# Two heads' rows in one transfer, and both pairs of batches through the first three layers before the last two

## The chip, the cores and the metric

The program runs on one core of one Trainium2 chip. The metric is the device time of one execution in microseconds. The kernel before has a median of 1160.0 us over three runs (1157.83 to 1166.39). The execution that was profiled took 1158.56 us, and its trace spans 1156.8 us of that. The mean clock granted to TensorE over the span was 0.984 of full speed.

## The reference

Inputs are float32, and the product accuracy asked for is close to float32's. Four batches of 448 tokens, 12 heads of 64:

```
scores = q @ k.T / sqrt(64) - log(448);  x = sigmoid(scores) @ v     # per batch and head
x  = x / sqrt(mean(x*x) + 1e-6) * rms_g                              # [1792, 768]
x  = (silu(x @ w_gate) * (x @ w_val)) @ w_out                        # 768 -> 1536 -> 768
h  = x @ w_in;   out = (h - tanh(h)) @ w_out2                        # 768 -> 2048 -> 768
```

The weights arrive as 64-bit words, which the kernel itself turns into float32 on the chip.

## The kernel before, in words

**Numbers in two parts.** A float32 operand is split into a high part (the value rounded to the matmul format fp32r) and a low part (value minus high part). A product of two operands is three matmuls: high by high, high by low, low by high. The splits are a cast (L279, on ScalarE "ACT" or VectorE "DVE") and a subtraction (L418, L459, L530, L670, L708, on DVE or GpSimd "POOL").

**Stages.** Attention comes first, pair of heads by pair of heads (24 pairs). For a pair, `pair_load` issues its DMAs, `pair_prep` splits q and k, `scores` makes the scores (L553), `sigmoid` runs on ACT (L563), `pair_av` multiplies with v (L593, L599). After each batch, `norm` makes the row norms. Then come the five weight matrices, called phases: Ag and Av (gate and value, L794), B (out, L830), C (in of the second block, L794), D (out of the second block, L830). All of this is done for batches 0 and 1, and then once more for batches 2 and 3.

**Jobs.** A and C phases use Strassen's seven products in Winograd's form on 2 by 2 blocks, where the two block columns are the two batches. One job is 63 matmuls. Its left factors are sums of weight blocks, made by `factors` (L413 the sums, L279 and L418 the splits). Its right factors are the sums B11, T1, T2, T3, B21, T4, B22 of pieces of x, made by `right_units` (L675 the sums, L670 the splits) for `i` = 0, 1, 2, each from two pieces m = 2i and 2i+1 of both batches. B and D phases are plain: a block is 6 matmuls, a group is four k by six m, so 24 blocks or 144 matmuls. In each group m goes up, and for each m the four k of the group come one after another. Each A and C job ends in evictions (L765) and the activation (L742, L743 for the gate; L746; L750, L751 for tanh), and then a split (L708) that gives one k for B or D. The evictions of B and D are L721.

**Weights.** `load` fetches 768 KB of raw words (L317). `convert` turns them into float32 by three ACT steps (L333, L338, L342; L336 on DVE instead of L338 in places) and two joins (L345 on DVE or POOL, L347 on DVE). Converted tiles are stored to DRAM for the second pair of batches and fetched from there (`fetch`, L392, L396). Six tiles of A are converted early, beside the attention. All the others of A, B, C and D are converted just ahead of the job that uses them, all within the passes of batches 0 and 1.

**What sets the order.** No engine queue is written by hand. The kernel records units of work in program order with `plan.add`, each with its engines, a guessed duration, what it reads and writes, and `after`, the guessed time from the end of a DMA's issue to its landing. `Plan.issue` then simulates the engines with these guesses. Of the units that could start within 300 ns of the soonest, it takes the one recorded first, and so writes one fixed instruction list per engine. At run time each engine works its list strictly in order and waits where an operand is late. All DMAs are issued by one engine, SyncE ("SP"). Buffers come from pools. The pool `wt` has 8 buffers, shared by raw words (at most 2), converted tiles (`whole` at most 2, `whl` at most 3) and left factors (`op`, at most 6).

**Second pair.** The attention output of batches 2 and 3 is spilled to DRAM (L623) and read back by `reload_x` (L662) during the last D group of batches 0 and 1. Beside that group, `right_a` also applies the norm (L697) and makes the right factors of the next A jobs.

Of the kernel before, what the change touches and what calls it, by code (L numbers as in the profile page):

```python
# [21 lines left out]
P = 128  # L22
# [4 lines left out]
GR = 4  # L27
# [9 lines left out]
N_UNIT, N_MOE, N_WT, N_CV = 81, 44, 8, 5  # L37
# [8 lines left out]
ORDER_1_OUT = [(k, m) for g in range(KF1 // GR) for m in range(KM) for k in range(g * GR, (g + 1) * GR)]  # L46
ORDER_2 = [(k, m) for m in range(KF2) for k in range(KM)]
ORDER_2_OUT = [(k, m) for g in range(KF2 // GR) for m in range(KM) for k in range(g * GR, (g + 1) * GR)]
# [13 lines left out]
class Plan:  # L62
# [7 lines left out]
    def __init__(self, room):  # L70
        self.room, self.work = room, []

    def add(self, engines, run, reads=(), writes=(), stream=None, after=0):

        n = len(self.work)
        self.work.append((engines, run, tuple(reads), tuple(writes), stream, after))
        for s, _ in (*reads, *writes):
            if not s.uses or s.uses[-1] != n:
                s.uses.append(n)

    def issue(self):
# [70 lines left out]
        while len(issued) < n_work:  # L152
# [25 lines left out]
            finish, start, n, e, ns, uses_port = min((c for c in cands if c[1] <= soonest), key=lambda c: c[2])  # L178
# [33 lines left out]
def tile_sigmoid_attention_moe_moe(  # L212
# [31 lines left out]
        "cv": (N_CV, {"cv": 2, "c": 2, "top": 1, "a22": 2}),  # L244
# [47 lines left out]
    for bs in BATCHES:  # L292
        for names, ph, n, order in ((FIRSTS[0], "B", KF1 // GR, ORDER_1_OUT), (FIRSTS[1], "D", KF2 // GR, ORDER_2_OUT)):
# [6 lines left out]
    early = [(ph, p) for ph, bs, p, blocks in jobs if blocks is None][:N_EARLY]  # L300


    turns = []
    for ph, p in early:
        turns += [(ph, 2 * p), (ph, 2 * p + 1)]
    for ph, bs, p, blocks in jobs:
        if bs == BATCHES[0] and (ph, p) not in early:
            turns += [(ph, p)] if blocks else [(ph, 2 * p), (ph, 2 * p + 1)]
# [3 lines left out]
    def load(i, reads=()):  # L312
# [4 lines left out]
        add({"SP": (2200, False)}, lambda e: nc.sync.dma_start(out=r.tile, in_=SRC[ph][at]), reads, [r["l"], r["h"]], after=2000)  # L317

    def convert(ph, at, word, c, x):
# [24 lines left out]
        def join():  # L344
            add({**dve(NW, fast=True), **pool1(NW)}, lambda e: ENG[e].tensor_scalar(  # L345
# [37 lines left out]
    def fetch(i):  # L383
# [4 lines left out]
        if blocks:  # L388
            if bs == BATCHES[0]:
                return  # L390
            d, w = stored.pop((ph, at)), slot("whl", wt_p, [P, 2, NW], F32R, "wt")
            add({"SP": (2200, False)}, lambda e: nc.sync.dma_start(out=w.tile.bitcast(F32), in_=d.tile), [d[x] for x in "hl"], [w["h"], w["l"]], after=2000)  # L392
            whls[i] = w
        elif bs == BATCHES[1] or (ph, at) in early:
# [51 lines left out]
    def whole_tile(i):  # L446

        ph, _, at, _ = jobs[i]
        c = slot("c", cv_p, [P, NW], U32, "cv")
# [481 lines left out]
    for j in range(len(jobs)):  # L931
        fetch(j + BACK)
        ahead = conv(j + AHEAD)
        for n, u in enumerate(job_units(j)):
# [8 lines left out]
            for f in ahead[lo:hi]:  # L943
                f()
# [60 lines left out]
```

## Time and profile before

| | |
|---|---|
| median of 3 runs | 1160.0 us (1157.83 to 1166.39) |
| profiled execution | 1158.56 us, span 1156.8 us |
| TensorE (PE) busy | 1107.9 us, 96% |
| VectorE (DVE) busy | 865.2 us, 75% |
| ScalarE (ACT) busy | 558.2 us, 48% |
| GpSimd (POOL) busy | 321.9 us, 28% |
| DMA | 162.27 MB, mean 140 GB/s |

A busy PE is not a PE at full pace. Matmuls overlap, so the pace is best read from how many stand in a stretch, and lost time from the spots where the next one starts late.

### The profile page before, as it was taken

To read this page: it belongs to the slowest core of one execution; us is meant where nothing else is said; L and a number is where in the kernel's file an instruction comes from. 1 tells how busy PE (TensorE), PEld (TensorE's weight loads), DVE (VectorE), ACT (ScalarE), POOL (GpSimd) and SP (SyncE) were. 2 spreads that over 40 slices of the span, in tenths; PEclk is the share of its full clock that TensorE was granted. 3 is DMA by queue.
4 is the path that set the end of the run, shared out by engine and by line. 5 is a ranking of instruction groups with operands and counts; after the bars stand their busy time and mean duration, and the time that the engine had idled before them with its cause. 6 is when DMAs were issued, how large, how long until landed. Compare 5 with 4: busy or idle time off the path is not lost. (4 is left out here: it accounts for less than half of the span.)

```text
span 1156.8 us, 15127 instructions
## 1 busy us (share of the span) xinstructions
PE 1107.9 (96%) x5574; PEld 943.8 (82%) x5574; DVE 865.2 (75%) x1347; ACT 558.2 (48%) x904; POOL 321.9 (28%) x203
## 2 busy tenths in 40 slices
PE   8798988999999997999999899999999999999998
PEld 4344443989999986899999789999999899999987
DVE  2566883796698899898999899948838899394642
ACT  4678996455476576676575424312303243121110
POOL 0003010253254232334444523322211324051300
PEclk9898999999999999999999899999999999999999
DMA  3777655234257463455556651221313113313203
GB/s 105 228 216 235 195 152 190 91 109 164 82 191 269 141 232 123 138 211 198 207 211 216 241 189 56 83 82 55 110 55 110 55 56 109 104 61 110 109 1 123
DMA packets 55322, 162.27 MB, mean 140 GB/s; under 512 B 13904, under 2 KB 30928, under 8 KB 55248
## 3 DMA queue, kind: packets, MB, share of 16 engines
q1 hardware_dynamic: 55248, 161.30, 41.4%
q8 instruction: 44, 0.72, 0.3%
q14 instruction: 30, 0.25, 0.1%
HBM read 115.27 MB, written 46.01 MB: 139 GB/s over the span
## 5 line engine op out<-in xcount | busy, mean ns | idle before, releaser
L794 PE MATMUL ps<-unit,wt 128*128 128x448 f32 x2160 | 454.9, 368 | 11.2 <-DVE unit L670 7.0
L794 PEld LDWEIGHTS ps<-unit,wt 128*128 128x128 f32 x2160 | 407.8, 189 | 49.6 <-DVE unit L670 7.8
L830 PE MATMUL ps<-unit,wt 128*128 128x448 f32 x2016 | 416.6, 367 | 8.2 <-DVE unit L279 7.3
L830 PEld LDWEIGHTS ps<-unit,wt 128*128 128x128 f32 x2016 | 379.7, 189 | 42.8 <-DVE unit L279 8.4
L765 DVE TENSOR_TENSOR unit<-ps,unit 128x448 f32<-128x448 f32 x240 | 142.6, 618 | 47.5 <-PE ps L794 44.0
L279 ACT COPY unit<-ps 128x448 f32<-128x448 f32 x86 | 45.8, 534 | 162.5 <-PE ps L794 90.0
L279 ACT CAST unit<-unit 128x448 fp32r<-128x448 f32 (+1 forms) x143 | 76.9, 567 | 86.0 <-DVE unit L721 22.0
L721 DVE TENSOR_TENSOR unit<-ps,unit 128x448 f32<-128x448 f32 x120 | 68.9, 616 | 60.9 <-PE ps L830 60.8
L345 POOL TENSOR_SCALAR cv<-cv 128x768 f32<-128x768 f32 x28 | 82.6, 2948 | 89.1 <-ACT cv L342 89.1
L563 ACT ACTIVATE unit<-ps 128x448 f32<-128x448 f32 x192 | 90.2, 543 | 5.4 <-PE ps L553 4.1
L279 ACT CAST wt<-cv 128x768 fp32r<-128x768 f32 x78 | 64.6, 833 | 57.2 <-PE ps L794 20.8
L553 PE MATMUL ps<-unit 64*128 64x448 f32 (+1 forms) x576 | 75.7, 397 | 14.3 <-ACT unit L279 5.0
L553 PEld LDWEIGHTS ps<-unit 64*128 64x128 f32 (+1 forms) x576 | 52.1, 182 | 42.9 <-issue 18.8
L794 PE MATMUL ps<-unit,cv 128*128 128x448 f32 x360 | 79.8, 366 | 0.0
L593 PE MATMUL ps<-unit 128*64 128x448 f32 x288 | 68.2, 607 | 9.3 <-ACT unit L563 9.2
L794 PEld LDWEIGHTS ps<-unit,cv 128*128 128x128 f32 x360 | 67.5, 188 | 5.6
L708 DVE TENSOR_TENSOR unit<-unit 128x448 fp32r<-128x448 f32 x89 | 66.5, 757 | 4.3 <-ACT unit L279 2.3
L418 POOL TENSOR_TENSOR wt<-cv,wt 128x768 fp32r<-128x768 f32 x21 | 41.6, 1980 | 100.2 <-ACT wt L279 56.7
L279 DVE CAST unit<-unit 128x448 fp32r<-128x448 f32 (+1 forms) x102 | 48.2, 473 | 28.2 <-DMA unit<-in_qkt 25.4
L342 ACT ACTIVATE cv<-wt 128x768 f32<-128x768 f32 x68 | 61.5, 906 | 10.5 <-DVE cv L347 3.9
L708 POOL TENSOR_TENSOR unit<-unit 128x448 fp32r<-128x448 f32 x23 | 26.8, 1169 | 138.0 <-DVE unit L279 130.2
L418 DVE TENSOR_TENSOR wt<-cv,wt 128x768 fp32r<-128x768 f32 x59 | 62.1, 1064 | 2.5 <-ACT wt L279 1.5
(71 smaller groups left out, 1020.7 us busy)
## 6 DMA issues: line engine op xcount, KB each, us to landing
wt<-in_w_out SPq DMA_DIRECT2D x28, 768.0 KB, 4.9
wt<-in_w_in SPq DMA_DIRECT2D x16, 768.0 KB, 5.9
wD<-wt SPq DMA_DIRECT2D x16, 768.0 KB, 4.1
wt<-wD SPq DMA_DIRECT2D x16, 768.0 KB, 4.2
wt<-in_w_gate SPq DMA_DIRECT2D x12, 768.0 KB, 5.4
wt<-in_w_val SPq DMA_DIRECT2D x12, 768.0 KB, 5.8
wB<-wt SPq DMA_DIRECT2D x12, 768.0 KB, 4.0
wt<-wB SPq DMA_DIRECT2D x12, 768.0 KB, 4.1
```

What stands on the lines that cost most here:

```text
L279: add(engines, lambda e: (nc.scalar.copy if e == "ACT" else nc.vector.tensor_copy)(to(), of()), reads, writes)
L342: add(act(NW), lambda e: nc.scalar.activation(t.tile, r.tile[:, :, 1].bitcast(F32), AF.Abs, scale=2.0 ** 16), [r["h"]], [t["t"]])
L345: add({**dve(NW, fast=True), **pool1(NW)}, lambda e: ENG[e].tensor_scalar(out=t.tile, in0=t.tile, scalar1=LOW, scalar2=HIGH, op0=ALU.max, ...
L418: add({**dve(n, psum=False), **pool(n)}, lambda e: ENG[e].tensor_sub(lo(), a(), hi().bitcast(F32)), [*ak, kh], [kl])
L553: nc.tensor.matmul(ps[i, c].tile[:n, :S], lhsT=f[w].tile[rows, c * P:c * P + n], rhs=f[q].tile[rows, :], start=(w, q) == ("kh", "qh"), sto ...
L563: add(act(S, psum=True), lambda e: nc.scalar.activation(to.tile[at:at + n, :S], ps.tile[:n, :S], AF.Sigmoid, bias=-math.log(S), scale=1.0 ...
L593: nc.tensor.matmul(ps.tile[i * D:(i + 1) * D, :S], lhsT=v.tile[:, n * D:(n + 1) * D], rhs=a.tile, start=(c == 0), stop=False)
L708: add({**pool(S), **dve(S, psum=False)}, lambda e: ENG[e].tensor_sub(c["l"].tile, t.tile, c["h"].tile.bitcast(F32)), [t["t"], kh], [kl])
L721: add(dve(S), lambda e: nc.vector.tensor_add(a.tile, psv(), a.tile), [ps["t"], a["t"]], [a["t"]])
L765: add(dve(S), lambda e: nc.vector.tensor_add(t.tile, banks[n].tile[:, :S], x.tile), [banks[n]["t"], x["t"]], [t["t"]])
L794: nc.tensor.matmul(ps.tile[:, :S], lhsT=part(a), rhs=x[b].tile, start=n not in ON_TOP and i == 0 and q == 0, stop=i == 2 and q == 2, skip_ ...
L830: nc.tensor.matmul(ps.tile[:, :S], lhsT=wt, rhs=a[p].tile, start=first and i == 0, stop=last and i == 2,)
```

## The change

The same numbers are computed, and the number of matmuls is the same. The parts:

1. **Loads of a pair of heads.** q and k of the two heads lie one after the other in DRAM, and now come as one DMA over 128 partitions instead of two over 64. Only the last 64 columns of k stay two DMAs in batches 0 and 1. v takes one DMA, its end one. A pair has 6 issues in batches 0 and 1 (9 before), 4 in batches 2 and 3 (10 before).
2. **Raw words.** The guess `after` of a raw load goes from 2000 to 3500 ns. The first raw loads no longer wait for the split of a pair.
3. **Order of phases.** Before: A and B, then C and D, for batches 0 and 1, then the same for 2 and 3. Now: A, B (0, 1), A, B (2, 3), C, D (2, 3), C, D (0, 1). The output of B for batches 0 and 1 is spilled and read back.
4. **Conversion of C.** All eight tiles of C are converted and stored beside the second pass of A and B (`later`, `steps`). D is converted in the pass of batches 2 and 3.
5. **Last group of B and D.** For m = 0 to 2 the first two k come for all three m, then the other two; m = 3 to 5 as before (`out_order`).
6. **Right factors after B.** `right_units` is cut in two parts, and for C these units rank 60 places earlier in the planner's choice. The first job of a phase does all products of i = 0 and 1 (save the one on top of another's bank) before any of i = 2.
7. **Silu.** The gate's sigmoid and multiplication become one Silu on ACT. The first limit of a conversion (L345) is on DVE alone. The pool `unit` has 79 buffers (81), `cv` 6 (5), of kind `c` 1 (2).

```
+FIRST = 60
+LEAD = {"A": BATCHES[0], "B": BATCHES[0], "C": BATCHES[1], "D": BATCHES[1]}
+def out_order(n):
+    half = GR // 2
+    order = [(k, m) for g in range(n // GR - 1) for m in range(KM) for k in range(g * GR, (g + 1) * GR)]
+    order += [(k, m) for ks in (range(n - GR, n - half), range(n - half, n)) for m in range(KM // 2) for k in ks]
+    return order + [(k, m) for m in range(KM // 2, KM) for k in range(n - GR, n)]
...
+        self.rank.append(n + self.lag)
-            finish, start, n, e, ns, uses_port = min((c for c in cands if c[1] <= soonest), key=lambda c: c[2])
+            finish, start, n, e, ns, uses_port = min((c for c in cands if c[1] <= soonest), key=lambda c: (self.rank[c[2]], c[2]))
...
-    for bs in BATCHES:
-        for names, ph, n, order in ((FIRSTS[0], "B", KF1 // GR, ORDER_1_OUT), (FIRSTS[1], "D", KF2 // GR, ORDER_2_OUT)):
+    for names, ph, n, order in ((FIRSTS[0], "B", KF1 // GR, ORDER_1_OUT), (FIRSTS[1], "D", KF2 // GR, ORDER_2_OUT)):
+        for bs in (LEAD[ph], *(x for x in BATCHES if x != LEAD[ph])):
...
+    first = [bs == LEAD[ph[0]] for ph, bs, _, _ in jobs]
+    early = FIRSTS[0][:N_EARLY]
+    later = FIRSTS[1]
...
-        add({"SP": (2200, False)}, lambda e: nc.sync.dma_start(out=r.tile, in_=SRC[ph][at]), reads, [r["l"], r["h"]], after=2000)
+        add({"SP": (2200, False)}, lambda e: nc.sync.dma_start(out=r.tile, in_=SRC[ph][at]), reads, [r["l"], r["h"]], after=3500)
...
-            add({**dve(NW, fast=True), **pool1(NW)}, lambda e: ENG[e].tensor_scalar(
+            add(dve(NW, fast=True), lambda e: ENG[e].tensor_scalar(
...
+            apart = w == "k" and hi > 3 * P and b < PAIRED
+            for i in range(2 if apart else 1):
+                rows = slice(i * D, (i + 1) * D) if apart else slice(0, P)
+                of = qk_rows[h * P + D:][rows, at + i * D:at + i * D + hi - lo]
...
+        if part == 0:
+            return [begin] + split("B11", "T1")
+        return [sums] + split("T2", "T3") + [rest] + split("B21", "T4", "B22")
...
-                xg[b, m] = a
-                if b % 2 and m % 2:
-                    for u in right_units("C", (b - 1, b), m // 2, xg):
+                xs[b, m] = xg[b, m] = a
+                if b not in LEAD["C"]:
+                    spill(b, m)
+                elif b % 2:
+                    plan.lag = -FIRST
+                    for u in right_units("C", (b - 1, b), m // 2, xg, m % 2):
                         u()
+                    plan.lag = 0
...
-            add(act(S, psum=psum), lambda e: nc.scalar.activation(sg.tile, of(), AF.Sigmoid), [x["t"]], [sg["t"]])
-            add(two, lambda e: ENG[e].tensor_mul(sg.tile, of(), sg.tile), [x["t"], sg["t"]], [sg["t"]])
+            add(act(S, psum=psum), lambda e: nc.scalar.activation(sg.tile, of(), AF.Silu), [x["t"]], [sg["t"]])
...
-    beside = [(last_c + 1, half_way, right_a(BATCHES[1], True))]
+    steps = [f for ph, p in later for f in both_halves(ph, p)]
+    beside = [(last["A"] + 1, starts["A", BATCHES[1]] - 1, right_all("A", BATCHES[1], True)),
+              (last["C"] + 1, starts["C", BATCHES[0]] - 1, right_all("C", BATCHES[0], True)),
+              (starts["A", BATCHES[1]], starts["C", BATCHES[1]] - 2, steps)]
```

What the planner makes of it is shown at three places. First ACT's list in the attention, from the second pair on. `L563 ACTIVATE` (`L585` in the changed kernel) are sigmoids, `L333` (`L345`) is the first step of a conversion, which needs raw words that have landed. Before:

```order
L279 COPY unit<-ps 128x448
L612 ACTIVATE unit<-unit 128x448
L563 ACTIVATE unit<-ps 128x448 x2
L563 ACTIVATE unit<-ps 64x448 x2
L563 ACTIVATE unit<-ps 128x448 x4
L279 COPY unit<-ps 128x448
L612 ACTIVATE unit<-unit 128x448
L333 ACTIVATE wt<-wt 128x768
```

Now:

```order
L585 ACTIVATE unit<-ps 128x448 x2
L585 ACTIVATE unit<-ps 64x448 x2
L585 ACTIVATE unit<-ps 128x448 x4
L291 COPY unit<-ps 128x448
L632 ACTIVATE unit<-unit 128x448
L585 ACTIVATE unit<-ps 128x448 x2
L585 ACTIVATE unit<-ps 64x448 x2
L585 ACTIVATE unit<-ps 128x448 x4
L345 ACTIVATE wt<-wt 128x768
```

The first conversion step stood behind 20 sigmoids and now stands behind 28, one pair later.

Second, SP's list at the start of the program, the first pair of heads. Before:

```order
L500 DMA unit<-in_qkt 64x128 x2
L500 DMA unit<-in_qkt 64x448 x2
L500 DMA unit<-in_qkt 64x256 x2
L500 DMA unit<-in_qkt 64x64 x2
L511 DMA unit<-in_vp 128x384
L520 DMA ve<-in_vp 64x64 x2
```

Now:

```order
L522 DMA unit<-in_qkt 128x128
L522 DMA unit<-in_qkt 128x448
L522 DMA unit<-in_qkt 128x256
L522 DMA unit<-in_qkt 64x64 x2
L540 DMA unit<-in_vp 128x384
L542 DMA ve<-in_vp 128x128
```

Eleven issues became seven. The first raw load stood behind 32 issues of q and k and now stands behind 21, after the same pair of heads.

Third, DVE's list where the last evictions of B (`L721`, now `L757`) lead to the right factors of C (`L675` and `L670`, now `L698` and `L693`). `L345`, `L347`, `L413` and `L418` are conversion and left factors. Before, for batches 0 and 1:

```order
L721 TENSOR_TENSOR unit<-ps,unit 128x448 x2
L345 TENSOR_SCALAR cv<-cv 128x768
L347 SCALAR_TENSOR_TENSOR wt<-cv,wt 128x768
L413 TENSOR_TENSOR cv<-wt 128x384
L413 TENSOR_TENSOR cv<-cv,wt 128x384
L413 TENSOR_TENSOR cv<-wt 128x384
L413 TENSOR_TENSOR cv<-wt,cv 128x384
L418 TENSOR_TENSOR wt<-wt 128x768
L675 TENSOR_TENSOR unit<-unit 128x448 x3
L670 TENSOR_TENSOR unit<-unit 128x448 x7
```

Now, for batches 2 and 3:

```order
L425 TENSOR_TENSOR cv<-wt,cv 128x384
L693 TENSOR_TENSOR unit<-unit 128x448
L430 TENSOR_TENSOR wt<-wt 128x768
L430 TENSOR_TENSOR wt<-cv,wt 128x2x384
L757 TENSOR_TENSOR unit<-ps,unit 128x448 x2
L698 TENSOR_TENSOR unit<-unit 128x448 x3
L693 TENSOR_TENSOR unit<-unit 128x448 x5
```

Seven DVE steps stood between the last evictions and the sums that C waits for, and now none does.

## Rows read from the trace of the kernel before

**Rows 1.** Stretches from start:end us (attention, first A+B, C+D, second A+B); columns as named

```profile
core 0: us, PE busy (x) PEld busy (x) DVE busy (x) ACT busy (x) POOL busy (x), PEclk, DMA share, GB/s
0.00:203.00 203.00, 177.22 (x1040) 89.96 (x1040) 120.58 (x219) 152.97 (x297) 19.01 (x19) 0.95 0.62 188
203.00:447.80 244.80, 243.20 (x1188) 221.25 (x1187) 204.00 (x315) 143.02 (x201) 93.23 (x54) 1.00 0.44 156
447.80:686.90 239.10, 225.95 (x1081) 207.15 (x1080) 217.75 (x321) 149.24 (x210) 94.89 (x49) 0.96 0.56 195
686.90:932.40 245.50, 241.96 (x1190) 222.96 (x1189) 188.25 (x287) 65.51 (x114) 66.66 (x48) 1.00 0.23 81
```

**Rows 2.** Timeline of PE, attention: start, us, what, [idle before, releaser]

```profile
5.87 1.49 PE L553 MATMUL ps<-unit 64*128 64x448 f32 x6 [1.53 <-DVE unit L279]
...
21.79 2.73 PE L553 MATMUL ps<-unit 64*128 64x448 f32 x24
...
27.75 2.73 PE L553 MATMUL ps<-unit 64*128 64x448 f32 x24
35.99 4.75 PE L593 MATMUL ps<-unit 128*64 128x448 f32 x12 [5.51 <-ACT unit L563]
...
41.67 2.69 PE L553 MATMUL ps<-unit 64*128 64x448 f32 x24
...
126.16 2.72 PE L553 MATMUL ps<-unit 64*128 64x448 f32 x24
...
132.17 2.72 PE L553 MATMUL ps<-unit 64*128 64x448 f32 x24
```

**Rows 3.** Timeline of ACT, attention, first steps of two conversions

```profile
34.61 0.89 ACT L333 ACTIVATE wt<-wt 128x768 uint32<-128x768 uint16 x1 [5.58 <-DMA wt<-in_w_gate]
...
181.29 0.89 ACT L333 ACTIVATE cv<-wt 128x768 uint32<-128x768 uint16 x1 [5.17 <-DMA wt<-in_w_out]
```

**Rows 4.** Timeline of SP, attention: issues of q and k, and of raw words

```profile
0.72 5.03 SPq L500 DMA_DIRECT2D unit<-in_qkt  x8
...
30.02 0.59 SPq L317 DMA_DIRECT2D wt<-in_w_gate  x1
```

**Rows 5.** Timeline of PE, A to D

```profile
459.77 6.32 PE L794 MATMUL ps<-unit,wt 128*128 128x448 f32 x20 [6.74 <-DVE unit L670]
...
486.66 8.72 PE L794 MATMUL ps<-unit,wt 128*128 128x448 f32 x34 [1.93 <-DVE wt L418]
...
657.81 29.27 PE L830 MATMUL ps<-unit,wt 128*128 128x448 f32 x131 [4.32 <-DVE unit L279]
...
693.79 0.47 PE L794 MATMUL ps<-unit,wt 128*128 128x448 f32 x1 [1.14 <-ACT unit L279]
...
932.38 9.28 PE L794 MATMUL ps<-unit,wt 128*128 128x448 f32 x45
```

**Rows 6.** What PE waited for, B and D: us in total, times, longest

```profile
PE ps L830 <- DVE unit L279: 7.3, 3, 4.3
```

**Rows 7.** The chain of waits, one undisturbed group of D: start, us, what

```profile
970.85 29.19 PE ps L830 x144
```

**Rows 8.** Timeline of DVE after the last evictions of the first B

```profile
451.98 1.15 DVE L721 TENSOR_TENSOR unit<-ps,unit 128x448 f32<-128x448 f32 x2
453.05 0.55 DVE L345 TENSOR_SCALAR cv<-cv 128x768 f32<-128x768 f32 x1
453.63 0.96 DVE L347 SCALAR_TENSOR_TENSOR wt<-cv,wt 128x768 uint32<-128x768 uint32 x1
...
457.50 1.69 DVE L675 TENSOR_TENSOR unit<-unit 128x448 f32<-128x448 f32 x3
```

**Rows 9.** Instructions by line and form: busy us, mean ns | idle before

```profile
L345 POOL TENSOR_SCALAR cv<-cv 128x768 f32<-128x768 f32 x28 | 82.6, 2948 | 89.1 <-ACT cv L342 89.1
...
L743 DVE TENSOR_TENSOR unit<-unit 128x448 f32<-128x448 f32 x27 | 20.1, 760 | 4.1 <-ACT unit L742 3.7
...
L888 ACT ACT_TABLE_LOAD x1 | 1.3, 1283 | 0.7 <-PEq L990 0.7
```

More of the change, by code (lines that the diff above doesn't have):

```diff
@@ L299, in tile_sigmoid_attention_moe_moe @@
                 at = to
[L300 to L308, printed above, removed]
+    first = [bs == LEAD[ph[0]] for ph, bs, _, _ in jobs]
+    early = FIRSTS[0][:N_EARLY]
+    later = FIRSTS[1]
+    ahead = set(early + later)
+    halves = lambda ph, p: [(ph, p)] if ph in "BD" else [(ph, 2 * p), (ph, 2 * p + 1)]
+    todo = [(ph, p) for (ph, _, p, _), f in zip(jobs, first) if f and (ph, p) not in ahead]
+    turns = [x for ph, p in early + [t for t in todo if t[0][0] in "AB"] + later + [t for t in todo if t[0][0] in "CD"] for x in halves(ph, p)]
     raws, whls, stored, ops, wholes = {}, {}, {}, {}, {}
@@ L470, in conv @@
         if blocks:
-            return whole_tile(i) if bs == BATCHES[0] else []
-        if bs == BATCHES[0] and (ph, at) not in early:
+            return whole_tile(ph, at, i) if first[i] and (ph, at) not in ahead else []
+        if first[i] and (ph, at) not in ahead:
             steps = {}
@@ L490, in pair_load @@
         t = qkr_t[b, p] = {w: unit("qkr") for w in "kq"}
-        def load(w, lo, hi, key):
-            for i in range(2):
-                rows = slice(i * D, (i + 1) * D)
-                of = qkt[b * H + 2 * p + i][rows]
-                at = lo + S * (w == "k")
-                if w == "k" and lo == 3 * P and b < PAIRED:
-                    at += i * D
-                add({"SP": (1.4 * (hi - lo), False)}, lambda e, of=of, rows=rows, at=at: nc.sync.dma_start(
-                    out=t[w].tile[rows, lo:hi], in_=of[:, at:at + hi - lo]), [], [t[w][key, lo, i]], after=2000)
@@ L522, in pair_prep @@
+        add({"SP": (460, False)}, lambda e: nc.sync.dma_start(out=to(), in_=rest), [], [end["t"]], after=2000)
     def pair_prep(b, p):
@@ L912, in tile_sigmoid_attention_moe_moe @@
     for i in range(2):
-        load(i, [pair_t[0, BEHIND]["ql"][0]] if (0, BEHIND) in pair_t else [])
+        load(i)
     cut = len(steps) * (len(one) - 8) // (len(one) + len(two) - 8)
     mixed(one[8:], steps[:cut])
-    mixed(two, right_a(BATCHES[0], False) + steps[cut:])
-    half_way = [j for j in range(len(jobs)) if jobs[j][1] == BATCHES[1]][0]
-    last_c = [j for j in range(half_way) if jobs[j][0] == "C"][-1]
+    mixed(two, right_all("A", BATCHES[0], False) + steps[cut:])
+    last, starts = {}, {}
+    for j, (ph, bs, _, blocks) in enumerate(jobs):
+        starts.setdefault((ph[0], bs), j)
+        if blocks is None and first[j]:
+            last[ph[0]] = j
     n_of = [len(blocks) if blocks else 21 for _, _, _, blocks in jobs]
@@ L932, in tile_sigmoid_attention_moe_moe @@
         fetch(j + BACK)
-        ahead = conv(j + AHEAD)
+        soon = conv(j + AHEAD)
         for n, u in enumerate(job_units(j)):
```

165 lines of the change are left out of this document (93 added, 72 removed).

## The prediction

> **What bounds the kernel now.** First read the stretches [rows 1]. From 203 us on, PE is busy for nearly the whole of each stretch, and DVE is the next fullest. It is busy 204.0 of 244.8 us in the first A and B and 217.8 of 239.1 us in the first C and D, but 188.3 of 245.5 us in the second A and B. Up to 203 us PE is busy for 177.2 us and no other engine is full, so that stretch loses time to waits. So the question is what PE's floor is and where it falls short of it.
>
> The pace comes from the chain of waits: 144 matmuls of D in 29.19 us, 0.2027 us each [rows 7]. The program has 4536 such matmuls in A to D (per pair of batches 20 jobs of 63 and seven groups of 144), so 919 us are fixed. A pair of heads that nothing disturbs takes 132.17 - 126.16 = 6.01 us [rows 2], 24 of them 144 us. The change removes no matmul, so it can only take away waits.
>
> In the attention two kinds of loss are large. The start: from the first scores at 5.87 to 21.79 us PE does one pair and a quarter, 7.5 us of work in 15.9, a loss of **8.4 us** [rows 2]. The other is ACT. It works its list in order, and at 34.61 us it had stood 5.58 us before the first step of a conversion whose raw words had not landed [rows 3]. They were issued at 30.02 us [rows 4], so they took 4.6 us, while sigmoids stood behind that step. PE then needed 41.67 - 27.75 = 13.9 us for that pair, 7.9 more than 6.01, since it also ran its next matmuls slowly [rows 2]. There are four such waits of ACT: 5.58 and 5.17 us [rows 3], and two more of 3.65 and 3.77 us between them. At 7.9 per 5.58 us, the 18.2 us of them cost PE **25.8 us**.
>
> In A to D, PE waits at few places [rows 5]. At 459.77, the start of the first C, it had waited 6.74 us for the split of a right factor, and then needed 6.32 us for 20 matmuls that take 4.1 at the pace above: **9.0 us**. At 486.66 it waited 1.93 us for a left factor and lost 1.8 to a slow pace: **3.7 us**. Three waits for the splits of the last k in the last group of B or D make 7.3 us [rows 6]. The longest, before 657.81, was followed by 131 matmuls in 29.27 us, 2.7 over the pace: together **10.0 us**. At 693.79, the start of the second A, it waited 1.14 us. The slow pace is the clock: the granted clock is 0.95 in the attention and 0.96 in the first C and D, 1.00 elsewhere [rows 1], and the slow matmuls follow PE's idle spots. So a wait that goes takes its slow stretch along.
>
> **The change part by part.**
>
> *Loads of a pair.* SP issues eight loads of q and k in 5.03 us, 0.63 each [rows 4]. The last q of the second pair was its 17th issue and is now its 11th, 3.8 us earlier. The start shrinks by at most that and by the slow matmuls in it: bounds 0 (the wider transfer lands later) and 6 us. I take **3.5**.
>
> *Conversions in the attention.* The first raw load went out at 30.02 us [rows 4] behind 46 issues, of which 32 are q and k. 14 issues fewer stand ahead of it, so it can go out some 9 us earlier, and its first step stands behind 28 sigmoids instead of 20, a pair of heads or 6 us later. Against a wait of 5.58 us this suffices, 7.9 us. For the other three waits the list gains only the 1.5 us of the longer guess and a shorter SP queue against 3.65 to 5.17 us. I take half of their 17.9. Together **17**, bounds 0 (the waits move to other steps) and 25.8.
>
> *Silu.* ACT has three table loads more. One takes 1283 ns [rows 9], two of them stand between the last sigmoids. Bounds 0 and 3.8 us of cost, I take **2**, since PE waits for ACT there. The Trainium skill, "ScalarE: Activation LUTs", section "What ACT_TABLE_LOAD costs", counts a drain of about 1380 ns with each load, 2.66 us per switch of set. By that rule the term would be 4 and the sum 2 us worse; the row here shows 1283 ns for the load alone. The multiplications that go (27 on DVE of 760 ns, 20.1 us in all [rows 9]) about pay for the 28 limits that come to DVE from POOL (2948 ns there [rows 9], 0.55 us on DVE [rows 8]). All this lies beside PE: 0.
>
> *Less slack on ACT.* It is busy 153.0 of 203 us [rows 1], and will be so in some 185. I take **1** off.
>
> *Start of C.* Between the end of the last evictions, 453.05 us, and the first sum of a right factor, 457.50 us, DVE did 4.4 us of conversion and left factors [rows 8], and these are now out of the way. The new order of the first job adds cover: 36 matmuls of i = 0 and 1 ahead of i = 2 instead of 24, 2.4 us. 4.4 + 2.4 covers the 6.74. The second C already has no such conversions, and its first 45 matmuls run through in 9.28 us, at the pace [rows 5]. Gain **9.0**, bounds 4 and 9.
>
> *Left factors of C.* C's tiles are converted a pass ahead: gain **3.2** of 3.7, bounds 0 and 3.7.
>
> *Last groups.* The late k was wanted after 12 matmuls and is now wanted after 36, 4.9 us later, more than the longest wait, 4.32 us [rows 5]. Gain **9.5**, bounds 6 and 10.
>
> *Start of A for batches 2 and 3.* This follows a pass with conversions now, where it followed one whose conversions were done. About 5 us of DVE work (two tiles of B) join the norm and the right factors in a stretch where PE already waited 1.14 us [rows 5]. Next late would be T2. Cost **1** more, bounds 0 and 7.
>
> *The `wt` buffers.* In the second A and B the conversion of C holds up to three of eight buffers (two of raw words, one tile). Cost **2**, bounds 0 and 10. C's conversion itself (16 steps on DVE of some 1.5 us, 0.55 + 0.96 [rows 8], 24 us) fits into the 57 us that DVE is idle there [rows 1]. The spills and reloads (12 more tiles each way) ride on DMA engines with a share of 0.23 in that stretch [rows 1]: 0. If that cover were gone, the right factors of C for batches 0 and 1 would be late.
>
> The sum: attention 3.5 + 17 - 2 - 1 = 17.5; A to D 9.0 + 3.2 + 9.5 - 1 - 2 = 18.7. Together 36.2 us off the profiled 1158.56, so **1122 us**. The profiled execution lies 1.4 us under the median of the runs, which is within their spread.
>
> **The rivals.**
>
> *The buffers run out (slower).* With three of eight `wt` buffers taken for the whole second A and B, the next tile of A can be fetched only when the last one is cut up, and each of the twelve A jobs there waits. From 3 us a job it eats the whole gain (36 of 36.2). At 5 us a job it gives 1182. Against it: in the first A and B the raw words share the same eight buffers, and PE was busy 243.2 of 244.8 us [rows 1]. Chance 0.06.
>
> *The attention stays as long.* ACT's steps are only shuffled, and the next late operand takes over: then only the 18.7 of A to D come, 1140. For it: ACT does the same work, plus table loads. Chance 0.17.
>
> *DVE is late for the new A start.* At the upper bound, 7 us of wait and 2 to 3 of slow pace behind it, as at 459.77 [rows 5]: 1132. Chance 0.14.
>
> *All the waits named go,* and nothing comes: 6 + 25.8 + 9 + 3.7 + 10 = 54.5, so 1104. Chance 0.08.
>
> *It does not do what it says.* The list is written from guessed durations, as it was before, and every wait above arose from such guesses. New ones of the same size may stand elsewhere: about 1152. Chance 0.06.
>
> **How the numbers follow.** The forecast has 0.49. The range from 1104 to 1147 takes in the forecast with its bounds and the two middle rivals. Outside it lie the first rival, the last one, and about half of the fourth: near 0.16, and with what I have not thought of near 0.2. One per cent, 11.6 us, is about what a measurement of this kernel can tell from no change. Faster by more (under 1148): 0.49 + 0.17 + 0.14 + 0.08, less 0.05 for the tails, 0.83. Within 1%: 0.10. Slower: 0.07.
>
> **What would show it.** In the timeline of ACT, no wait of over 2 us before the first step of a conversion up to the last sigmoid. The first A job would start in earnest near 185 us instead of 203. The first C would follow B without a wait of PE, and no last group would show a wait of over 1 us. The start of A for batches 2 and 3 is where I expect the longest wait that is left. It would be wrong if ACT still waits for raw words, if PE's busy share in the second A and B falls under that of the first, or if the waits of PE for DVE add up to 20 us again.

## The result, and the profile after

The changed kernel takes 1112.65 us (1111.61 to 1126.05, 4 runs) against 1158.91 us (1155.02 to 1166.39) for the kernel before on the same chip: ratio 0.962, 95% interval 0.9532 to 0.9708. The execution that was profiled is the longest of the four, 1126.05 us; what its extra 13 us are is told below. Medians and intervals here and below leave out an execution more than 1.5% above the fastest of its kernel, which concerns one of x6_sigmoid.

PE's floor has not moved, so the gain must stand in the places where PE fell short of it. First the stretches (start:end in us, then busy time of each engine), in the new order of phases: attention, A and B for batches 0 and 1, A and B for 2 and 3, C and D for 2 and 3, C and D for 0 and 1. They answer to [rows 1].

```profile
core 0: us, PE busy (x) PEld busy (x) DVE busy (x) ACT busy (x) POOL busy (x), PEclk, DMA share, GB/s
0.00:194.80 194.80, 181.87 (x1125) 99.98 (x1126) 130.52 (x248) 164.91 (x313) 10.82 (x15) 0.98 0.60 199
194.80:425.50 230.70, 226.73 (x1109) 208.86 (x1108) 190.31 (x295) 126.90 (x180) 57.71 (x42) 0.99 0.52 182
425.50:672.00 246.50, 244.63 (x1178) 221.91 (x1177) 188.52 (x294) 108.74 (x165) 45.13 (x36) 0.99 0.46 157
672.00:900.00 228.00, 228.00 (x1104) 206.86 (x1103) 194.44 (x296) 116.05 (x175) 64.36 (x46) 1.00 0.44 157
900.00:1124.00 224.00, 220.31 (x1067) 199.75 (x1065) 131.62 (x198) 44.08 (x77) 50.01 (x35) 1.00 0.25 86
```

The attention is shorter and fuller, and its granted clock is 0.98 instead of 0.95. The first C and D, behind the attention once the stretch with the most waits and with a clock of 0.96, is now 228.00 us of busy PE in 228.00 us.

**Attention.** PE's timeline (start us, us, engine, line, what, and in brackets the idle time before and who ended it), to be held against [rows 2]:

```profile
4.31 4.07 PE L575 MATMUL ps<-unit 64*128 64x448 f32 x24
10.20 2.43 PE L575 MATMUL ps<-unit 64*128 64x448 f32 x12 [1.83 <-DVE unit L291]
...
16.54 2.73 PE L575 MATMUL ps<-unit 64*128 64x448 f32 x24
...
22.51 2.72 PE L575 MATMUL ps<-unit 64*128 64x448 f32 x24
...
194.82 1.46 PE L833 MATMUL ps<-unit,cv 128*128 128x448 f32 x6
```

The pair whose scores began at 21.79 begins at 16.54, and no pair takes 13.9 us any more. 194.82 is the first A matmul behind the last one of the attention. In the kernel before that place reads

```profile
210.25 2.06 PE L794 MATMUL ps<-unit,cv 128*128 128x448 f32 x9
```

Some A matmuls are done earlier, in the gaps of the attention: 45 of them before, 87 now. Taking each off at 0.2027 us [rows 7] leaves 201.1 and 177.2 us: the attention gave **23.9 us**. The experiments below are compared by this number.

Why can be read from SP and ACT. SP's timeline, for [rows 4]:

```profile
0.74 2.57 SPq L522 DMA_DIRECT2D unit<-in_qkt  x5
...
19.85 0.91 SPq L329 DMA_DIRECT2D wt<-in_w_gate  x2
```

The first raw words go out at 19.85 instead of 30.02 us. Added up over the timeline of SP, the issues of the attention fall from 274 with 152 us to 165 with 76 us. ACT's timeline, for [rows 3], shows the first step of the first conversion with no wait in front of it, and then the three table loads that Silu brings:

```profile
27.36 0.92 ACT L345 ACTIVATE wt<-wt 128x768 uint32<-128x768 uint16 x1
...
179.05 1.28 ACT L782 ACT_TABLE_LOAD   x1
181.28 0.58 ACT L782 ACTIVATE unit<-unit 128x448 f32<-128x448 f32 x1 [0.94 <-DVE unit L804]
181.87 1.28 ACT L585 ACT_TABLE_LOAD   x1
183.17 1.96 ACT L585 ACTIVATE unit<-ps 128x448 f32<-128x448 f32 x4
185.14 1.28 ACT L782 ACT_TABLE_LOAD   x1
```

No wait of ACT for raw words is left in the attention; the longest there before was 5.58 us.

**A to D.** The same view of PE, for [rows 5]:

```profile
388.85 14.76 PE L870 MATMUL ps<-unit,wt 128*128 128x448 f32 x72
404.52 7.74 PE L870 MATMUL ps<-unit,wt 128*128 128x448 f32 x36 [0.92 <-ACT wt L291]
414.33 1.08 PE L870 MATMUL ps<-unit,wt 128*128 128x448 f32 x4 [2.07 <-DVE wt L291]
416.39 8.31 PE L870 MATMUL ps<-unit,wt 128*128 128x448 f32 x32 [0.98 <-DVE wt L478]
424.54 5.03 PE L833 MATMUL ps<-unit,wt 128*128 128x448 f32 x24
429.40 1.38 PE L833 MATMUL ps<-unit,cv 128*128 128x448 f32 x6
432.65 7.35 PE L833 MATMUL ps<-unit,wt 128*128 128x448 f32 x27 [1.87 <-DVE unit L757]
439.84 0.78 PE L833 MATMUL ps<-unit,cv 128*128 128x448 f32 x3
...
643.82 29.92 PE L870 MATMUL ps<-unit,wt 128*128 128x448 f32 x144
673.58 5.12 PE L833 MATMUL ps<-unit,wt 128*128 128x448 f32 x24
...
867.19 29.92 PE L870 MATMUL ps<-unit,wt 128*128 128x448 f32 x144
896.95 5.12 PE L833 MATMUL ps<-unit,wt 128*128 128x448 f32 x24
```

The last groups (643.82, 867.19) and the starts of C (673.58, 896.95) run through. One place loses time: the last B group of batches 0 and 1 and the start of A behind it. From 388.85 to 439.84 stand 72 + 36 + 4 + 32 + 24 + 6 + 27 = 201 matmuls, 40.7 us at 0.2027, in 51.0 us: **10.2 us**. To add up A to D, I take from start to start of matmuls what is over the pace. That makes 28.2 us before and 10.5 now, a gain of **17.7**.

The two gains make 41.6 us, but the profiled executions differ by 1158.56 - 1126.05 = 32.5. The rest is a second pace of the matmuls. Two undisturbed groups of B in the chain of waits of this execution, to be held against [rows 7]:

```profile
241.27 29.19 PE ps L870 x144
...
493.32 29.76 PE ps L870 x144
```

29.19 us are 0.2027 us a matmul, 29.76 are 0.2067. From some 437 us to the end every matmul of this execution runs at the second pace, which costs 13.2 us; in the execution before it was 4.0. 41.6 - 13.2 + 4.0 = 32.4, which closes the account.

### The profile page after: what moved, and what is told of

It is laid out like the page before. It is cut to its first block, busy times and chain, and to the rows that moved or that the text cites. A ratio compares the mean times of both kernels' runs of the same rounds, so it can differ in the third digit from the quotient of the medians.

```text
span 1124.3 us, 14971 instructions
## 1 busy us (share of the span) xinstructions
PE 1101.5 (98%) x5574; PEld 937.4 (83%) x5574; DVE 835.4 (74%) x1327; ACT 560.7 (50%) x909; POOL 228.0 (20%) x173
## 4 chain that ended last, share of the span: by engine, by line
PE 90%; ACT 5%; DVE 3%; issue 1%; DMA 0%; SPq 0%; POOL 0%; DVEq 0%; ACTq 0%; POOLq 0%
PE ps L833 46%; PE ps L870 36%; PE ps L613 3%; PE ps L575 3%; ACT unit L585 2%; PE ps L619 1%; ACT unit L291 1%; DVE unit L693 1%; DVE unit L733 0%; ACT cv L354 0%; ACT wt L345 0%; DVE unit L757 0%; SPq L522 0%; ACT unit L632 0%; DVE unit L552 0%
## 5 line engine op out<-in xcount | busy, mean ns | idle before, releaser
L291 ACT COPY unit<-ps 128x448 f32<-128x448 f32 x88 | 46.5, 533 | 175.8 <-PE ps L833 107.1
L291 ACT CAST unit<-unit 128x448 fp32r<-128x448 f32 x140 | 75.7, 565 | 77.3 <-DVE unit L698 24.7
L757 DVE TENSOR_TENSOR unit<-ps,unit 128x448 f32<-128x448 f32 x120 | 68.8, 615 | 60.4 <-PE ps L870 60.3
L585 ACT ACTIVATE unit<-ps 128x448 f32<-128x448 f32 x192 | 90.3, 542 | 9.7 <-PE ps L575 8.5
L291 ACT CAST wt<-cv 128x768 fp32r<-128x768 f32 x75 | 62.2, 833 | 58.6 <-PE ps L833 26.3
L575 PE MATMUL ps<-unit 64*128 64x448 f32 (+1 forms) x576 | 72.5, 390 | 5.7 <-ACT unit L291 2.4
L744 DVE TENSOR_TENSOR unit<-unit 128x448 fp32r<-128x448 f32 x94 | 73.5, 788 | 4.1 <-ACT unit L291 2.3
L613 PE MATMUL ps<-unit 128*64 128x448 f32 x288 | 61.2, 557 | 1.7 <-ACT unit L585 1.7
L425 POOL TENSOR_TENSOR cv<-wt 128x384 f32<-128x384 f32 x30 | 37.8, 1265 | 123.1 <-DVE wt L359 54.0
L291 DVE CAST unit<-unit 128x448 fp32r<-128x448 f32 (+2 forms) x105 | 50.2, 478 | 16.8 <-DMA unit<-in_qkt 13.4
L430 DVE TENSOR_TENSOR wt<-cv,wt 128x768 fp32r<-128x768 f32 x61 | 58.5, 967 | 3.4 <-ACT wt L291 2.4
L430 POOL TENSOR_TENSOR wt<-cv,wt 128x768 fp32r<-128x768 f32 x19 | 37.3, 1968 | 113.1 <-ACT wt L291 102.4
L357 DVE TENSOR_SCALAR cv<-cv 128x768 f32<-128x768 f32 x68 | 41.1, 604 | 22.3 <-ACT cv L354 22.1
```

The costliest lines, as they stand in the source:

```text
L291: add(engines, lambda e: (nc.scalar.copy if e == "ACT" else nc.vector.tensor_copy)(to(), of()), reads, writes)
L357: add(dve(NW, fast=True), lambda e: ENG[e].tensor_scalar(out=t.tile, in0=t.tile, scalar1=LOW, scalar2=HIGH, op0=ALU.max, op1=ALU.min), [t[ ...
L430: add({**dve(n, psum=False), **pool(n)}, lambda e: ENG[e].tensor_sub(lo(), a(), hi().bitcast(F32)), [*ak, kh], [kl])
L575: nc.tensor.matmul(ps[i, c].tile[:n, :S], lhsT=f[w].tile[rows, c * P:c * P + n], rhs=f[q].tile[rows, :], start=(w, q) == ("kh", "qh"), sto ...
L585: add(act(S, psum=True), lambda e: nc.scalar.activation(to.tile[at:at + n], ps.tile[:n, :S], AF.Sigmoid, bias=-math.log(S), scale=1.0 / ma ...
L613: nc.tensor.matmul(ps.tile[i * D:(i + 1) * D, :S], lhsT=v.tile[:, n * D:(n + 1) * D], rhs=a.tile, start=(c == 0), stop=False)
```

## The experiments

Each is compared by its time and by two numbers of its one trace: the attention (in us, as above) and what A to D lose over the pace of their place, be it the first or the second. Two traces of the changed kernel differ by 3.2 us in the first and 0.7 in the second. Before is 1160.02 us (11 runs), 1159.56 (7) or 1157.57 (7), by session, and each ratio is against its own.

| | median us (range) | ratio, 95% | attention | lost |
|---|---|---|---|---|
| before, first session | 1158.91 | 1 | 201.1 | 28.2 |
| the change, first session | 1112.65 (1111.61 to 1126.05) | 0.9532 to 0.9708 | 177.2 | 10.5 |
| x1_again | 1118.38 (1112.02 to 1122.92) | 0.9606 to 0.9667 | 180.4 | 9.8 |
| x2_guess2000 | 1115.52 (1113.59 to 1120.71) | 0.9590 to 0.9649 | 181.0 | 10.8 |
| x3_loads_apart | 1145.86 (1140.78 to 1154.87) | 0.9842 to 0.9924 | 207.7 | 11.2 |
| x10_two_queues | 1127.78 (1123.66 to 1134.65) | 0.9669 to 0.9776 | 188.3 | 9.8 |
| x4_attention_alone | 1135.57 (1135.33 to 1137.42) | 0.9763 to 0.9819 | 173.3 | 31.7 |
| x5_plain_groups | 1127.73 (1127.29 to 1131.21) | 0.9714 to 0.9772 | 179.8 | 21.9 |
| x9_c_in_its_pass | 1125.11 (1118.86 to 1129.21) | 0.9657 to 0.9758 | 174.1 | 16.9 |
| x7_no_rank | 1122.78 (1115.91 to 1125.35) | 0.9614 to 0.9714 | 179.3 | 11.1 |
| x6_sigmoid | 1118.87 (1116.93 to 1124.27; its trace: 1136.24) | 0.9628 to 0.9712 | 177.8 | 20.6 |
| x8_b_tiles_early | 1115.82 (1108.83 to 1118.61) | 0.9579 to 0.9670 | 176.8 | 7.4 |
| x11_pool_again | 1112.80 (1109.09 to 1118.01) | 0.9531 to 0.9647 | 179.3 | 8.8 |
| x12_b_pool | 1124.24 (1119.60 to 1127.70) | 0.9636 to 0.9731 | 179.0 | 19.7 |

**x1_again: the changed kernel, unchanged, once more.**

> The changed kernel once more. Theory: PE's matmuls of A to D have two paces, 0.2027 and 0.2067 us, and a wait of PE can leave it at the slower one until a later wait. Then runs lie near 1112 us (0.2027 throughout) or up to 14 us above it (about 3400 matmuls at 0.2067), and the profile of a run of each kind shows that pace in its timeline. Rival: the extra 14 us of the profiled execution were waits of its own (late DMAs); then a run near 1112 and one near 1126 differ in PE's waits and not in the pace.

Its profiled execution took 1115.39 us, with the first pace in all of it. The same group in its chain of waits:

```profile
493.87 29.18 PE ps L870 x144
```

One program, one place, 29.18 and 29.76 us: the second pace comes without any change of the kernel, and the rival, waits of its own, does not make these 13 us. Against the first execution it saves the 13.2 us of pace and 0.7 in A to D and loses 3.2 in the attention: 10.7 us, the difference of 1126.05 and 1115.39. Its own account against the kernel before is 20.7 + 18.4 + 4.0 = 43.1 us, against 1158.56 - 1115.39 = 43.2.

### Where the attention's gain comes from

**x2_guess2000: the guess for raw words as it was.**

```
-        add({"SP": (2200, False)}, lambda e: nc.sync.dma_start(out=r.tile, in_=SRC[ph][at]), reads, [r["l"], r["h"]], after=3500)
+        add({"SP": (2200, False)}, lambda e: nc.sync.dma_start(out=r.tile, in_=SRC[ph][at]), reads, [r["l"], r["h"]], after=2000)
```

> The changed kernel with the guess for the landing of raw words back at 2000 ns. Theory that the loads (14 issues fewer ahead of the first raw words) took ACT's waits away: in the attention the first steps of conversions stand at the same places, no wait of ACT for raw words over 2 us, the last scores of the attention within 3 us of the changed kernel's, 1112 to 1118 us. Theory that the longer guess took them away: at least two waits of ACT of 3 us or more before such a step, 1122 to 1132 us.

1115.52 us, attention 181.0 against 177.2 and 180.4: beside the wide loads the guess does nothing that can be seen. The first steps of the conversions keep their places, and ACT still waits for no raw words.

**x3_loads_apart: two transfers per pair of heads again,** with the guess of 3500 and all else of the change.

```
-            for i in range(2 if apart else 1):
-                rows = slice(i * D, (i + 1) * D) if apart else slice(0, P)
+            for i in range(2):
+                rows = slice(i * D, (i + 1) * D)
...
```

> The changed kernel with two transfers for the two heads of a pair again (9 and 10 issues a pair), the guess kept at 3500 ns. Theory that SP's issues were the limit: the start is 4 to 5 us later, ACT waits for raw words at one or two places for 2 to 4 us each, 1120 to 1130 us. Theory that the guess suffices: only the start comes back, 1115 to 1118 us.

1145.86 us and an attention of 207.7: it lost 27 us or more, over all that the attention had gained. The theory named the cause and was far too low in its price (1120 to 1130). ACT's timeline has the waits again:

```profile
35.15 0.89 ACT L345 ACTIVATE wt<-wt 128x768 uint32<-128x768 uint16 x1 [2.36 <-DMA wt<-in_w_gate]
...
63.83 0.89 ACT L345 ACTIVATE wt<-wt 128x768 uint32<-128x768 uint16 x1 [4.59 <-DMA wt<-in_w_val]
...
113.23 0.89 ACT L345 ACTIVATE wt<-wt 128x768 uint32<-128x768 uint16 x1 [4.99 <-DMA wt<-in_w_gate]
```

A longer guess did not save it. But two things return with the narrow loads: SP's issues (274 with 157 us), and shorter runs in DRAM with more packets. The next run parts them.

**x10_two_queues: x3 with the second transfer of each two on POOL's queue.**

```
-                add({"SP": (1.4 * (hi - lo), False)}, lambda e, of=of, rows=rows: nc.sync.dma_start(
+                add({"POOL" if i else "SP": (1.4 * (hi - lo), False)}, lambda e, of=of, rows=rows: ENG[e].dma_start(
...
```

> Two transfers per pair of heads again, as in the run with the loads apart (1145.9 us, attention 27 us longer), but the second of each two is issued by POOL, so that SP has no more issues in the attention than the changed kernel. Theory (what the wide loads save is SP's time for issuing): raw words are issued on time again, no wait of ACT for them over 2 us, and the time comes back to 1116 to 1128; POOL's own issues may cost a few us. Rival (it is the transfers themselves, shorter runs and more packets on the DMA engines): ACT waits for raw words as before, and the time stays at 1140 to 1150.

The transfers are those of x3, yet 18.1 of its us are gone, and the attention is 19.4 us shorter; the time is at the upper end of the theory's range. SP has 166 issues with 88 us there, POOL the other 109. The waits of ACT for raw words that are left:

```profile
19.46 0.89 ACT L345 ACTIVATE wt<-wt 128x768 uint32<-128x768 uint16 x1 [2.15 <-DMA wt<-in_w_gate]
...
94.30 0.91 ACT L345 ACTIVATE wt<-wt 128x768 uint32<-128x768 uint16 x1 [1.36 <-DMA wt<-in_w_val]
```

One is just over the 2 us that the theory allowed. A rival is left: that a second queue makes raw words land faster. It does not. Here are SP's first raw load and the median from issue to landing of a raw load of the gate (KB each, us), first of x3, then of x10:

```profile
30.69 0.59 SPq L329 DMA_DIRECT2D wt<-in_w_gate  x1
wt<-in_w_gate SPq DMA_DIRECT2D x12, 768.0 KB, 5.1
...
14.92 0.58 SPq L329 DMA_DIRECT2D wt<-in_w_gate  x1
wt<-in_w_gate SPq DMA_DIRECT2D x12, 768.0 KB, 6.7
```

A raw load takes longer to land in x10, and the waits go because it is issued earlier. So what the wide loads save is mostly SP's time: with it taken by other loads, raw words go out late. 8 to 11 us of attention against the wide loads remain. Of these one part can be named: ACT waits 6.9 us for q and k of the first pairs (what ACT waited for: us in total, times, longest), which is 0 and 1.9 us in the two traces of the changed kernel.

```profile
ACT unit L291 <- DMA unit<-in_qkt: 6.9, 2, 3.6
```

The large transfers of q and k (96 and 112 KB) land 4.2 to 4.4 us after their issue there by the median, on either queue, and 2.7 to 3.2 us after it in x3. What makes them slower stays open.

**x4_attention_alone: the kernel before with the new loads and the guess,** nothing else.

> The kernel before with the new loads and the new guess alone; order of phases, Silu and the rest as before. Theory that the two parts of the gain (some 24 us in the attention, some 18 in A to D) are independent: 1131 to 1138 us, attention as in the changed kernel, PE's waits in A to D near 28 us in all. Rival: an earlier end of the attention runs into weights that are not ready, and the gain is lost in the first A: over 1145 us.

1135.57 us. The attention has all of its gain and more (173.3, which is 4 to 7 us less than in the changed kernel), and A to D lose 31.7 us, about as in the kernel before. So the gain in the attention doesn't need the rest of the change. Which of the other parts takes 4 to 7 us of it back, no run shows.

### Where the gain in A to D comes from

**x5_plain_groups: the last groups in the old order.**

```
+    return [(k, m) for g in range(n // GR) for m in range(KM) for k in range(g * GR, (g + 1) * GR)]
```

> The changed kernel with the last group of B and D in the order of the other groups (k within m). PE's lost time in A to D (time over the pace of 0.2027 to 0.2067 us a matmul) is 9.8 to 10.5 us in the changed kernel. Theory that the order of the last group hides the late k: waits of 1 to 4 us come back about 12 matmuls into the last groups, lost time 15 to 21 us, 1119 to 1127 us. Rival, that DVE has got enough slack by the other parts: lost time under 13 us, within 3 us of the changed kernel.

1127.73 us, just over the theory's range, and 11.4 us more are lost than in the first trace of the changed kernel, 11.2 of them at the three last groups that had no loss. What PE waited for in B and D (us in total, times, longest) has [rows 6] again, and a wait of ACT's:

```profile
PE ps L867 <- DVE unit L288: 3.7, 3, 2.0
PE ps L867 <- ACT unit L288: 2.9, 1, 2.9
```

**x9_c_in_its_pass: C converted in C's own pass** (`later = []`).

> The changed kernel with C converted in the pass of batches 2 and 3, just ahead of its jobs, instead of beside the second A and B. Theory that conversion on DVE between the last evictions of B and the right factors made the 9.0 and 3.7 us at the first C: waits of 4 to 13 us come back within 40 us of the start of C, lost time in A to D 14 to 24 us, 1117 to 1128 us. Rival, that the rank and the order of the first job suffice: lost time under 12 us.

The wait at the start of the first C is back, 6.3 us with the slow matmuls behind it (PE's timeline):

```profile
682.58 0.47 PE L833 MATMUL ps<-unit,wt 128*128 128x448 f32 x1 [3.89 <-ACT unit L291]
683.59 5.06 PE L833 MATMUL ps<-unit,wt 128*128 128x448 f32 x17 [0.54 <-DVE unit L693]
```

In DVE's timeline conversion and left factors (L357, L359, L425, L430) stand from 673.52 to 680.65 us, with one eviction among them, and the last eviction and the sums come behind them. The other wait at the first C, for a left factor (3.7 us before), does not come back: from 685 us on PE waits for nothing in this trace.

**x7_no_rank: `FIRST = 0`,** so that the sums for C have no lead in the list.

> The changed kernel without the lead of 60 places that the sums of the right factors of C for batches 2 and 3 have in the list. Theory (C's start lost its wait because the conversions and left factors of C had gone out of the way): the lead only reorders steps that DVE has time for, PE waits under 1 us at the start of C, and the time stays within 0.5% of the changed kernel, 1112 to 1118. Rival (the lead is what pays): the wait at the start of C for batches 2 and 3 is there again with 4 to 9 us, 1118 to 1125, as in the run where C's tiles are converted in C's own pass.

Both signs of the theory were missed, and one of the rival's: in the trace 2.0 us are lost at the start of C (0 and 1.1 in the changed kernel's two traces), over the 1 us of the theory and under the 4 of the rival, and the median, 1122.78, lies in the rival's range. The profiled execution took 1115.91, the others 1122.53 to 1125.35. With ten executions of the changed kernel between 1111.61 and 1126.05 the times decide nothing; the trace, as far as it goes, speaks for conversions, and the lead may be worth 1 to 2 us.

**x6_sigmoid: sigmoid and a multiplication instead of Silu.**

> The changed kernel with the gate's sigmoid and multiplication in two steps instead of Silu: three table loads fewer on ACT, 48 multiplications more on DVE or POOL. Theory that the loads stand on the path at the end of the attention: last matmul of the attention 2 to 4 us earlier, lost time in A to D up to 3 us more; 1109 to 1116 us. Rival, that DVE's steps count: lost time in A to D 5 us or more over the changed kernel's, 1118 to 1124 us.

Its interval overlaps that of x1_again, and the attention is not shorter without the table loads (177.8). The theory's 1109 to 1116 us was missed. The execution that was traced took 1136.24 us, 12 us over the next; it loses 11.8 us at the start of the second A (8.6 and 10.2 in the two traces with Silu) and 7.9 near 480, all waits for DVE, and some 13 us are the second pace. It does not stand for the other three, so what the 36 multiplications that DVE has there cost is not shown, and the times don't settle whether Silu is worth anything.

### The 10 us that are left

In the stretch of these waits DVE has next to no gap (columns as in the first view). The second line is one of the two short stretches behind waits in which the granted clock is 0.50, 1.2 GHz:

```profile
391.00:436.00 45.00, 39.16 (x177) 34.54 (x176) 43.62 (x71) 16.16 (x28) 8.90 (x6) 0.94 0.48 172
433.80:437.20 3.40, 3.40 (x11) 3.01 (x10) 2.75 (x5) 0.53 (x1) 0.00 (x0) 0.50 0.45 166
```

43.62 of 45.00 us, and PE waits there for tiles of B (L291, L478) and an eviction (L757). All but the first of these waits, 5.0 of 5.9 us, end with a step of DVE's. The first, 0.92 us, ends with a cast on ACT, which by ACT's timeline had itself waited 1.65 us for PE's matmuls, so it is no wait for DVE. The two stretches at half the clock add some 3 us to the loss.

**x8_b_tiles_early: B's last two tiles, 10 and 11, converted beside the last jobs of A.**

```
+    moved = {FIRSTS[0][9]: ("B", 10), FIRSTS[0][10]: ("B", 11)}
```

> The changed kernel with the last two tiles of B converted beside the A jobs of the last group and fetched back, instead of beside the right factors of the second A. Theory that DVE's list is what PE waits for in that last group (DVE has no gap from 391 to 436 us in the profile of the change): about 5 us of steps leave it, the lost time there falls from 10 to 5 us or less; 1105 to 1112 us. Rival, that the fetched tiles and the eight buffers bring waits in place of these: lost time in A to D 9 us or more.

The waits for tiles shrink to 1.1 us, and new ones stand 65 us on (PE's timeline):

```profile
396.83 1.08 PE L874 MATMUL ps<-unit,wt 128*128 128x448 f32 x4 [0.92 <-ACT wt L291]
398.08 21.36 PE L874 MATMUL ps<-unit,wt 128*128 128x448 f32 x104 [0.17 <-DVE wt L482]
...
463.95 2.09 PE L837 MATMUL ps<-unit,wt 128*128 128x448 f32 x9 [1.73 <-DVE unit L808]
468.22 2.09 PE L837 MATMUL ps<-unit,wt 128*128 128x448 f32 x9 [2.18 <-DVE unit L808]
```

DVE works off left factors (L429, L434) and C's conversions (L361, L363) there, and evictions (L808) stand in its list behind them. So the loss at the old place goes as the theory said, and about half of it comes back elsewhere: 7.4 us lost instead of 9.8 to 10.5. The time, above the 1105 to 1112 of the theory, can't be told from the changed kernel's.

**x11_pool_again and x12_b_pool: the limit of a conversion may go to POOL again,** in the changed kernel and in x8.

```
-            add(dve(NW, fast=True), lambda e: ENG[e].tensor_scalar(
+            add({**dve(NW, fast=True), **pool1(NW)}, lambda e: ENG[e].tensor_scalar(
```

> The changed kernel, with the limit to the range of the low words allowed on POOL again, as in the kernel before. Some 22 steps of 0.55 us go from DVE to POOL. Theory (the 10 us that PE loses at the end of the last B group of batches 0 and 1 are a queue on DVE, which works there without a gap): the loss shrinks by the steps that leave this stretch, 1 to 4 us of 10, and the time is 1108 to 1117. Rival (a step on POOL takes some 3 us, and the chain of a tile gets that much longer): tiles come later, new waits of 2 to 5 us, 1118 to 1130.

> B's tiles 10 and 11 converted beside the last jobs of A, as in the run with B's tiles early, and the limit allowed on POOL again. With the tiles early alone the waits in the last B group were gone, but PE waited 4.5 us near 465 us for DVE, which worked off C's conversions there. Theory (DVE's queue): with two limits or so on POOL in that stretch the 4.5 us go to 0 to 3, and the time is 1108 to 1114. Rival (longer chains through POOL): the loss from 200 us on stays at 7 us or grows, 1115 to 1128.

In the changed kernel all 68 limits are on DVE (lines and forms: busy us, mean ns, idle time before), where [rows 9] had 28 on POOL at 2948 ns:

```profile
L357 DVE TENSOR_SCALAR cv<-cv 128x768 f32<-128x768 f32 x68 | 41.1, 604 | 22.3 <-ACT cv L354 22.1
```

In x11, 26 steps leave DVE, and A to D lose 8.8 us instead of 9.8 to 10.5: 1112.80 us, level with the changed kernel. In x12 PE waits for left factors of the new A,

```profile
435.94 1.86 PE L837 MATMUL ps<-unit,cv 128*128 128x448 f32 x4 [5.00 <-DVE cv L434]
```

and loses 19.7 us, 1124.24. In the first the time fits the theory, but 1 to 2 us are little more than two traces of one kernel differ by, so the theory isn't shown; in the second it failed, and the rival's price came. That POOL's steps stand in the late chain there is my reading; no run takes them out one by one. No version beats the changed kernel by more than can be measured.

## Why the prediction was right, step by step

The sum was 36.2 us off the profiled 1158.56; the result's two medians are 46 apart, its profiled executions 32.5 and 43.2. At equal pace the traces give 39 to 42 us. 1112.65 is inside the range, 9 below the forecast. 3 to 6 of these 9 us are the attention, sized too low; another 4 are the second pace, which stood in the profiled execution that the sum started from and which the sum did not know.

- **Start of the attention**, 3.5 with 0 to 6: 21.79 to 16.54, 5.3 us. Near its upper bound.
- **Conversions**, 17 of 25.8: the attention's gain of 20.7 to 23.9 us less 5.3 leaves 15 to 19 for this term with Silu and slack in it, for which the sum had 14. Loads and guess alone gave 27.8 (x4), where the sum had 20.5, and the other parts took 4 to 7 of that back, where it had 3: part of the agreement is two errors that offset each other. In its reason the term was only half right. I let all of the first wait go and half of the others, which had "only the 1.5 us of the longer guess and a shorter SP queue". The guess is worth nothing (x2), and the shorter queue nearly everything (x3, x10): SP spent 152 of some 210 us on issuing, and every raw load of the attention stood behind that, not the first alone. All waits went.
- **Silu**, 2: nothing that can be seen. By the rows it is 1.28 us a load and no more: the sigmoid begins 0.02 us after its load, and the load 0.01 us after the activation ahead of it. The rule that the prediction weighed, a drain with each load (the Trainium skill, "ScalarE: Activation LUTs", "What ACT_TABLE_LOAD costs"), doesn't show here; the trace decides for the row. PE has no wait from 170 to 200 us. The 27 multiplications that the prediction set against the limits are one form of them; the same view has 12 more on DVE (7.4 us).
- **Start of C**, 9.0: right. It is 0 to 1.1 us now, and comes back with 6.3 when C's conversions do (x9). The other 2.7 fit the 2.4 us of cover from the new order of the first job, which no run takes out alone. That the lead in the list had a part isn't shown (x7).
- **Left factors of C**, 3.2: all 3.7 went, but not for the reason given. With C converted in its own pass again no wait for a left factor comes back (x9); what took it away stays open. **Last groups**, 9.5: all went at the three groups behind the first B (11.1 us by the account), and x5 brings 11.2 back at the same three.
- **Start of A for batches 2 and 3**, 1 with 0 to 7: the term of A to D that was most mis-sized. 10.2 us are lost (8.6 in x1_again) where the kernel before lost 3.1 (1.2 in the last B group and 1.9 at the second A), so it costs 5.5 to 7.1; some 3 of the 10.2 are lost at half the clock. I had named the place and DVE's 5 us for two tiles of B, but read the price off the wait that stood there (1.14 us, [rows 5]) and off the cover of a whole stretch, in which DVE is busy 204.0 of 244.8 us [rows 1]. The row that I should have asked for is the end of that stretch in the kernel before:

```profile
425.00:452.00 27.00, 27.00 (x135) 25.03 (x134) 26.20 (x44) 18.22 (x28) 7.12 (x4) 1.00 0.38 131
```

  26.20 of 27.00 us: there is no room. The change takes C's work out of this place and brings A's. In these 27 us conversion and left factors of C (L345, L347, L413, L418) are some 8 us of DVE; in the changed kernel the norm of the new A alone is 8.5 us of the 45 from 391 to 436 (L733); right factors stand in both. So DVE stays full, with B's tiles among it. Taken by place, the end of the first B with what follows it lost 10.2 us before (1.2, then the 9.0 at the first C) and loses 8.6 to 10.2 now: the loss that went at C's start is met again at A's. What was late were B's own tiles and an eviction, not T2 as I wrote. x8, which moves these tiles, takes most of the loss away from there, so they are the cause shown for it; how DVE's time there divides among the others isn't. The rival "DVE late for the new A start" had mechanism and price; it came beside the other gains and not in place of them.
- **The `wt` buffers**, 2: nothing. The second A and B has PE busy for 244.63 of 246.50 us, and the waits in it are those above. The rival of 1182 falls with that.
- **Attention stays as long** (1140): x3 is what that looks like, 1145.86.

So the attention was sized 3 to 6 us too low (17.5 against 20.7 to 23.9), and A to D about right (18.7 against 17.7 and 18.4) by errors of both signs, which is luck: 9.0 + 3.7 + 11.1 = 23.8 us stood at the places where I expected 21.7 to go, another 1.3 went at a wait in the first A that I had not named, and the new start of A and the buffers cost 5.5 to 7.1 instead of 3.

## What to carry to other kernels

An issue queue is an engine like the others: add up its issues over a stretch before pricing a late transfer, and cut their number before tuning guesses. When steps are moved into a stretch, read the busy share of the engine that runs them in that stretch alone, tens of us and not a phase, and set what leaves the stretch against what comes. Before an account is closed to a few us, count matmuls against the pace in each execution; the pace itself may differ.

## What the runs showed that I had not expected

The two paces. Both stand at a granted clock of 1.00, 2.4 GHz (stretches of the profiled execution of the changed kernel, columns as in the first view):

```profile
241.30:270.40 29.10, 29.10 (x145) 26.97 (x144) 18.19 (x28) 16.58 (x25) 0.00 (x0) 1.00 0.64 217
493.30:523.00 29.70, 29.70 (x146) 26.97 (x145) 14.91 (x23) 7.04 (x13) 2.66 (x2) 1.00 0.52 185
```

The difference of 2% comes and goes within executions of one program, in these traces each time where a matmul starts late (here behind the wait at 430 us and the stretch at half the clock that ends at 437), and can stay for hundreds of us. All 4536 matmuls at the second pace instead of the first would be 18 us, more than most terms of the sum. What sets it, no run here shows.
